# A state-space convolution followed by a gated MLP: the K matmul's moving operand laid out anew, the parameter loads split by chunk, and the order of work before the loop changed

## The chip, the cores and the metric

One core of one Trainium2 chip. The time is device microseconds of one execution, and lower is better. The kernel before takes 380.85 us (median of 16 executions, 379.3 to 383.0). TensorE (PE in the profile) does the matmuls, VectorE is DVE, ScalarE is ACT, GpSimd is POOL.

## The reference

```python
def _A_ref(u, A_re, A_im, B_re, B_im, C_re, C_im, log_dt, Dskip):   # u: 1 x 2048 x 640, parameters 640 x 192
    dt = jnp.exp(log_dt)[:, None]
    logdA = dt * (A_re + 1j * A_im)
    dB = dt * (B_re + 1j * B_im)
    l = jnp.arange(L)
    P = jnp.exp(logdA[:, :, None] * l[None, None, :])
    K = jnp.einsum("dn,dnl,dn->dl", Cc, P, dB).real
    ...                                     # y = causal convolution of u with K along L, by FFT
    return y + u * Dskip

h = x + _A_ref(_layernorm(x), ...)                                   # x is A_u
h2 = h + (silu(_layernorm(h) @ w1) * (_layernorm(h) @ w3)) @ w2      # 640 -> 1536 -> 640
```

All inputs and the output are bf16.

## The kernel before

The work falls into three parts. First, for three chunks of channels (256, 256 and 128 of the 640), the kernel K is built: with a tap number l = 16 j + i, `at` holds w z^j and `bt` holds exp(alpha i), and `k_mm` multiplies them so that the sum over n is the matmul's contraction. `k_evac` (ACT) takes the product from PSUM, and `k_dft` transforms it to frequencies. Secondly, the first tiles of the layer norm and of the transform of u are made. Thirdly, a loop over eight tiles does the inverse transform, the second layer norm and the MLP.

I call what belongs to the K matmuls of chunk 0, 1 and 2 stage 0, 1 and 2. ACT and DVE build the operands of one stage while PE multiplies those of the stage before. `w_mul` makes w, and `w_lanes` (ACT, after transposes on PE) copies it to where `at` needs it. `a_chain` (DVE) builds `at` in five steps, which I call a-steps. `b_first` and `b_rest` (ACT) and `b_mul` (DVE) build `bt`. `kf_evac` takes the frequencies from PSUM, product(c) multiplies those of tile c with those of K, and `h_add` adds a tile's result to the residual.

The matmul and its eviction:

```python
def k_mm(h, at, bt, kc, b):
    ...                                                   # x = cw // 8, 48 for a chunk of 256
        la = mkap(at[p0:p0 + pn], part * JJ * cw + col, [[astr, pn], [x, P]])
        rb = mkap(bt[p0:p0 + pn], part * II * CWM + col, [[bstr, pn], [x, 2], [CWM, II], [2 * x, 4]])
        T.matmul(pk[:, half, gi * P:(gi + 1) * P], lhsT=la, rhs=rb, ...)
    ...                                                   # 32 matmuls make one block

def k_evac(h, pk, kc, b):
    for c2 in range(2):
        src = pk[:].rearrange("p h (g c x) -> p h g c x", g=4, c=2)[:, :, :, c2, :]
        ...
        S.mul(out=dst, in_=src, mul=mask[:, c2:c2 + 1])
```

`la` is the stationary operand and `rb` the moving one. The innermost step of `rb` is 2x = 96 elements.

The order of the program (in the traces each engine's instructions stand in this order: DVE in the kernel before has alpha(0) at 10.04 us, w_mul(0) at 11.53, alpha(1) at 18.51):

```python
alpha(0)                            # DVE: alp = dt * (A_re, A_im), in lanes, from PSUM
c_scale(0); c_scale(1); c_scale(2)  # ACT: csd = dt * C
ze0 = z_exp(0)
w_mul(0, V); w_mul(2, G)            # w = (dt C) B: chunk 0 on DVE, chunk 2 on GpSimd
zs0 = z_sin(0); w_lanes(0)
alpha(1); alpha(2); tables()
b_first(0, bt0, "sin")              # ACT
z_mul(0, zs0, ze0)                  # DVE from here
...                                 # two a-steps, w_mul(1), third a-step, b_mul(0)
for b in range(nb[0]):              # stage 0: four blocks
    pk = k_mm(0, at0, bt0, kc, b)
    if b < len(IGS):
        stg.append(b_rest(1, bt1, "sin", IGS[b]))    # ACT: operands of stage 1
    k_evac(0, pk, kc, b)
...                                 # a_chain(1) on DVE
pb = k_dft(0, kc)
kf_evac(0, pb, "SSSS")
...
zs2 = z_sin(2); b_first(2, bt2, "sin")               # ACT: operands of stage 2
stg = [b_rest(2, bt2, "exp", ig) for ig in IGS]
...
warm(30, at1[:, 0:512])             # 30 dummy matmuls
for b in range(nb[1]):              # stage 1: four blocks
    pk = k_mm(1, at1, bt1, kc, b)
    k_evac(1, pk, kc, b)
pb = k_dft(1, kc)
...                                 # stage 2, layer norm of tiles 0 and 1, k_dft(2)
run(product(0))
...                                 # first inverse tiles, h_add and norm, twice
run(product(1))
for c in range(2, NPRE + 1):
    lst[c] = ln1_stats(c, G)
    if c < NPRE:
        ulns[c] = ln1_apply(c, lst[c]); skip(c, ulns[c])
        for f in range(NFT): fwd_evac(c, f, fwd_mm(ulns[c], f))
for c in range(NC):                 # the loop
    ...
```

## Time and profile before

| | before |
|---|---|
| median, us | 380.85 (16 executions) |
| profiled execution, us | 380.38 (span of the trace 378.4) |
| mean granted TensorE clock | 0.864 |
| PE / DVE / ACT / POOL busy, us | 308.6 / 267.1 / 155.1 / 36.8 |

The shares are averages over stages with different limits, so the reading goes by stretches. Here is the busy time by stretch for stage 0, the stretch before the loop, and the loop. The columns are the stretch in us, its length, then the busy time and the number of instructions of PE, of PE's weight loads, of DVE, ACT and POOL, then the granted clock, the DMA share and GB/s.

```profile
54.82:77.70 22.88, 22.88 (x128) 13.55 (x129) 22.67 (x35) 19.32 (x40) 0.00 (x0) 0.50 0.00 1
147.50:179.50 32.00, 10.77 (x63) 6.26 (x60) 27.10 (x79) 6.47 (x11) 1.56 (x8) 0.69 0.20 62
179.50:378.00 198.50, 188.33 (x1607) 154.40 (x1604) 139.42 (x309) 51.91 (x84) 27.98 (x96) 1.00 0.04 14
```

In stage 0 PE is full, but DVE (22.67 of 22.88) and ACT (19.32) nearly are as well: if PE gets faster there, the others take over soon. In the second stretch only DVE is nearly full. The third is PE's.

### The profile page before, as it was taken

The numbers are of one execution on the slowest core, as the hardware profiler recorded it, in microseconds if no ns is written. First come the engines' busy times: TensorE is split into PE (matmuls) and PEld (weight loads), VectorE is DVE, ScalarE is ACT, GpSimd is POOL, SyncE is SP. The second block draws the span as 40 slices with busy tenths as digits, with TensorE's granted clock in tenths as the row PEclk, the third lists the DMA queues.
The fourth block names the chain that finished last, engine by engine and source line by source line (L and its number), as shares of the span: only waits on it lengthen the run. The fifth ranks groups of instructions, "written<-read, shape, count | busy, mean of one in ns | idle before, by whom it ended". The sixth has DMA issues, their size and how long they took to land.

```text
span 378.4 us, 7036 instructions
## 1 busy us (share of the span) xinstructions
PE 308.6 (82%) x2907; PEld 227.6 (60%) x2907; DVE 267.1 (71%) x584; ACT 155.1 (41%) x317; POOL 36.8 (10%) x124
## 2 busy tenths in 40 slices
PE   1424929989998898204989989989899899998996
PEld 0212315574656656102877878868778778787884
DVE  3589999986994003897687888888879586783222
ACT  2999999818931134102351240421503402213030
POOL 1400000000000000001140230220321101001000
PEclk9999965556855559955999999999999999999999
DMA  8846000000004702400000001000000010000100
GB/s 185 283 126 126 2 0 0 2 2 3 0 3 131 289 0 75 138 0 0 3 1 36 2 0 36 0 9 30 1 19 17 2 36 0 20 17 2 36 0 35
DMA packets 12009, 15.74 MB, mean 42 GB/s; under 512 B 4426, under 2 KB 10570, under 8 KB 11850
## 3 DMA queue, kind: packets, MB, share of 16 engines
q1 hardware_dynamic: 10000, 14.57, 12.4%
q10 hardware_dynamic: 1978, 0.74, 0.8%
q8 instruction: 22, 0.36, 0.4%
q14 instruction: 9, 0.07, 0.1%
HBM read 12.42 MB, written 2.88 MB: 40 GB/s over the span
## 4 chain that ended last, share of the span: by engine, by line
PE 71%; DVE 20%; ACT 3%; DMA 3%; issue 1%; POOL 0%; ACTq 0%; DVEq 0%
PE ps L566 25%; PE ps L296 15%; PE ps L579 14%; PE ps L325 5%; PE ps L531 4%; PE ps L402 3%; DMA par_bi<-in_A_B_im_dram 3%; DVE st L374 3%; PE ps L343 2%; DVE at L279 2%; DVE at L274 2%; DVE tt L276 2%; ACT sg L571 1%; ACT kc L314 1%; DVE xl L545 1%
## 5 line engine op out<-in xcount | busy, mean ns | idle before, releaser
L571 ACT ACTIVATE sg<-ps 128x512 bf16<-128x512 f32 x48 | 28.7, 597 | 131.9 <-PE ps L566 131.9
L296 PE MATMUL ps<-bt,at 128*128 128x128 bf16 (+1 forms) x320 | 57.3, 406 | 7.7 <-DVE bt L260 7.7
L566 PE MATMUL ps<-xt,w1sb 128*128 128x256 bf16 x480 | 60.5, 273 | 0.0
L566 PE MATMUL ps<-xt,w3sb 128*128 128x256 bf16 x480 | 60.2, 273 | 0.0
L572 DVE TENSOR_TENSOR hm<-sg,ps 128x512 bf16<-128x512 bf16 x48 | 32.9, 685 | 36.1 <-ACT sg L571 35.7
L579 PE MATMUL ps<-w2sb,hm 128*128 128x320 bf16 x384 | 53.5, 299 | 0.0
L296 PEld LDWEIGHTS <-at 128*128 128x128 bf16 (+1 forms) x320 | 34.0, 148 | 30.5 <-DVE bt L260 8.2
L566 PEld LDWEIGHTS <-w1sb 128*128 128x128 bf16 x480 | 46.9, 98 | 7.3
L566 PEld LDWEIGHTS <-w3sb 128*128 128x128 bf16 x480 | 47.0, 98 | 5.4
L579 PEld LDWEIGHTS <-hm 128*128 128x128 bf16 x384 | 37.6, 98 | 14.2
L402 PE MATMUL ps<-uln,ft 128*128 128x320 bf16 x128 | 23.5, 332 | 12.4 <-DVE uln L387 11.3
L365 POOL TENSOR_TENSOR ta<-rs 128x2 f32<-128x2 f32 x26 | 7.4, 285 | 228.7 <-DVE rs L363 227.7
L374 DVE BATCH_NORM_STATS2 st<-xs 128x6 f32<-128x320 bf16 x64 | 27.9, 477 | 0.5
L409 ACT CAST vt<-ps 128x640 bf16<-128x640 f32 x32 | 20.9, 694 | 14.9 <-PE ps L402 14.9
L402 PEld LDWEIGHTS <-ft 128*128 128x128 bf16 x128 | 13.4, 107 | 19.8 <-DVE uln L387 11.6
L586 DVE TENSOR_TENSOR ot<-ps,xs 128x640 bf16<-128x640 f32 x16 | 13.2, 824 | 15.7 <-PE ps L579 15.7
L314 ACT ACTIVATE kc<-ps,mask 128x512 bf16<-128x512 f32 x20 | 12.6, 682 | 23.5 <-PE ps L296 23.4
L325 PE MATMUL ps<-kc,wt 32*128 32x64 bf16 (+1 forms) x768 | 18.6, 264 | 4.2 <-ACT kc L314 2.7
L343 PE MATMUL ps<-at,ident 128*128 128x512 bf16 x70 | 19.3, 446 | 2.5 <-DVE at L279 2.5
L338 DVE CAST kf<-ps 128x128 bf16<-128x128 f32 x2 | 0.5, 286 | 29.2 <-ACT kf L336 29.2
L325 PEld LDWEIGHTS <-wt 32*128 32x128 bf16 x768 | 17.8, 115 | 5.4 <-issue 5.4
L231 ACT ACTIVATE bt<-alp 128x384 bf16<-128x384 f32 (+1 forms) x45 | 20.8, 461 | 0.0
(104 smaller groups left out, 398.5 us busy)
## 6 DMA issues: line engine op xcount, KB each, us to landing
xs<-in_A_u_dram SPq DMA_DIRECT2D x4, 640.0 KB, 9.8
out_dram<-ot SPq DMA_DIRECT2D x16, 160.0 KB, 1.8
wt<-ftd SPq DMA_DIRECT2D x4, 512.0 KB, 6.7
w1sb<-in_B_w_dram SPq DMA_DIRECT2D x1, 1920.0 KB, 8.7
w3sb<-in_B_w_dram SPq DMA_DIRECT2D x1, 1920.0 KB, 13.1
w2sb<-in_B_w_dram SPq DMA_DIRECT2D x1, 1920.0 KB, 9.6
ftd<-ft SPq DMA_DIRECT2D x1, 256.0 KB, 2.6
par_ar<-in_A_A_re_dram SPq DMA_DIRECT2D x1, 240.0 KB, 5.7
```

Source lines behind the costliest of these rows:

```text
L231: S.activation(out=dst, in_=alp[h][:, 1, :], func=ACT.Sin, scale=-float(i))
L296: T.matmul(pk[:, half, gi * P:(gi + 1) * P], lhsT=la, rhs=rb, start=first, stop=last, tile_position=((p0, 0) if n1 else None), skip_group_ ...
L314: S.mul(out=dst, in_=src, mul=mask[:, c2:c2 + 1])
L325: T.matmul(pb[blk][:, f * 2 * cg:(f + 1) * 2 * cg], lhsT=wt[32 * blk:32 * blk + 32, i, f * P:(f + 1) * P], rhs=rb, start=(i == 0 and f == ...
L343: T.matmul(pw[:, 0, :], lhsT=ident[:], rhs=rhs, start=True, stop=True)
L374: V.bn_stats(out=st[:, q, :], in_=src[:, q * (D // 2):(q + 1) * (D // 2)])
L402: T.matmul(pv[:, q, 0:D // 2], lhsT=ft[:, k, f * P:(f + 1) * P], rhs=uln[:, k, q * (D // 2):(q + 1) * (D // 2)], start=(k == 0), stop=(k = ...
L409: S.copy(out=vts[c][:, f // 2, f % 2, :].rearrange("p (q d) -> p q d", q=2), in_=pv[:, :, 0:D // 2])
L566: T.matmul(pg[:, b, u * TB:(u + 1) * TB], lhsT=w[:, kt, fb * P:(fb + 1) * P], rhs=xts[c][:, kt, :], start=(kt == 0), stop=(kt == DT - 1))
L571: S.activation(out=sg[:], in_=pg[:, 0, :], func=ACT.Silu)
L572: V.tensor_tensor(out=hms[c][:, 2 * fp:2 * fp + 2, :], in0=sg[:].rearrange("p (u t) -> p u t", u=2), in1=pg[:, 1, :].rearrange("p (u t) -> ...
L579: T.matmul(po[:, q, 0:D // 2], lhsT=hms[c][:, fb, k * P:(k + 1) * P], rhs=w2sb[:, fb, q * (D // 2):(q + 1) * (D // 2)], start=(fb == 0), s ...
```

## The change

The intent has four parts. (1) The channels of a group are laid side by side in `bt`, so that the K matmul's moving operand reads eight neighbours at a time. This needs `alp` in a second order (a second pass of `alpha` for chunks 0 and 1) and makes `k_evac` read every second f32. (2) The loads are split by chunk, chunk 0 first, and c_scale(0) goes from ACT to GpSimd, so that the work starts earlier; on DVE, alpha(1) and alpha(2) move behind the first two a-steps, and the third a-step moves ahead of w_mul(1). (3) The 30 dummy matmuls go, the 40 ahead of stage 0 become 24 that stand earlier in the program but run later, since they read the last a-step and a part of `bt` that is multiplied late, and ACT builds stage 2's operands ahead of `kf_evac(0)`. (4) The statistics of tiles 2 and 3 move ahead of product(0), and the transform of tile 2 goes between the two `h_add`s.

The diff, cut to its core:

```diff
-    for nm, src, q in (("ar", A_A_re, nc.sync), ("cr", A_C_re, nc.scalar), ...):
-        q.dma_start(out=t[:], in_=src.rearrange("(s p) n -> p s n", p=P))
+    for h, cd in enumerate(CHUNKS):
+        nc.scalar.dma_start(out=ldcol[:, s0:s0 + ns], in_=A_log_dt[...].rearrange("(p s) -> p s", s=ns))
+    load(nc.sync, "ar", 0)
+    load(nc.sync, "ai", 0)
+    load(nc.scalar, "cr", 0)
+    load(nc.scalar, "ci", 0)
+    load(nc.sync, "br", 0)
+    load(nc.sync, "bi", 0)
+    for h in (1, 2):
+        for nm in ("ar", "ai", "cr", "ci", "br", "bi"):
+            load(nc.sync, nm, h)
...
-                S.mul(out=csd[:, part, s, :], in_=par[nm][:, s, :], mul=dtcf[:, s:s + 1])
+                if h == 0:
+                    G.tensor_scalar(out=csd[:, part, s, :], in0=par[nm][:, s, :], scalar1=dtcf[:, s:s + 1], ...)
+                else:
+                    S.mul(out=csd[:, part, s, :], in_=par[nm][:, s, :], mul=dtcf[:, s:s + 1])
...
-            rb = mkap(bt[p0:p0 + pn], part * II * CWM + col, [[bstr, pn], [x, 2], [CWM, II], [2 * x, 4]])
+            rb = mkap(bt[p0:p0 + pn], part * II * CWM + 8 * col, [[bstr, pn], [CWM, II], [1, 8]])
...
-            src = pk[:].rearrange("p h (g c x) -> p h g c x", g=4, c=2)[:, :, :, c2, :]
+            src = pk[:].rearrange("p h (g x c) -> p h g x c", g=4, c=2)[:, :, :, :, c2]
...
-    alpha(0)
+    alpha(0, "(m g)")
     c_scale(0)
+    ze0 = z_exp(0)
+    w_mul(0, V)
+    alpha(0, "(g m)")
+    zs0 = z_sin(0)
+    w_lanes(0)
     c_scale(1)
     c_scale(2)
...
-    alpha(1)
-    alpha(2)
...
     at0 = run(a0, 2)
+    alpha(1, "(m g)")
+    alpha(2, "(g m)")
+    run(a0, 1)
     inverse_table()
     w_mul(1, V)
+    alpha(1, "(g m)")
...
+    warm(14, last_a(0, at0))
+    warm(10, bt0[:, 0, IGS[1][-1], 0:CWM])
...
-    warm(40, at0[:, 0:512])
...
+    zs2 = z_sin(2)
+    bt2 = b_tile(2)
+    b_first(2, bt2, "sin")
     pb = k_dft(0, kc)
     kf_evac(0, pb, "SSSS")
...
-    zs2 = z_sin(2)
-    bt2 = b_tile(2)
-    b_first(2, bt2, "sin")
...
-    warm(30, at1[:, 0:512])
...
     pb = k_dft(2, kc)
+    skip(0, ulns[0])
+    ulns[1] = ln1_apply(1, lst[1])
+    lst[2] = ln1_stats(2, G)
+    skip(1, ulns[1])
+    lst[3] = ln1_stats(3, G)
...
         tr_evac(0, k, tp)
+        if k == 0:
+            ulns[2] = ln1_apply(2, lst[2])
+            for f in range(NFT):
+                fwd_evac(2, f, fwd_mm(ulns[2], f))
     run(product(1))
-    for c in range(2, NPRE + 1):
...
+    skip(2, ulns[2])
```

## The prediction

> **What bounds the kernel now.** I read the page's slices first (is one engine always the bound?), then the chain that ended last in order of time, then the timeline and the busy time by stretch where the chain changes engine.
>
> ```profile
> PE   1424929989998898204989989989899899998996
> DVE  3589999986994003897687888888879586783222
> ACT  2999999818931134102351240421503402213030
> PEclk9999965556855559955999999999999999999999
> ```
>
> One digit is 9.46 us. After slice 19 (180 us) PE is full at full clock: 199 us of matmuls that the diff leaves alone. Before it there are four stages with different bounds: ACT and DVE both full (slices 1 to 5), PE at half clock (6 to 15), then DVE with PE empty (16 to 18). The chain, cut to its large pieces:
>
> ```profile
> 2.33 9.85 DMA par_bi<-in_A_B_im_dram
> ...
> 22.02 1.50 DVE zs L212 x3
> ...
> 54.82 22.94 PE ps L296 x125
> 77.78 1.28 ACT kc L314 x2
> 79.10 7.24 PE ps L325 x256
> 86.34 8.96 PE ps L343 x30
> 95.31 22.75 PE ps L296 x121
> ...
> 128.33 11.40 PE ps L296 x63
> ...
> 148.27 0.82 DVE z L516
> ...
> 175.07 4.45 PE ps L402 x16
> ```
>
> So the end is set in turn by the parameter load; DVE without a gap from 22.02 to 54.8; the K matmuls (L296), 57.1 us in three stages; 8.96 us of dummy matmuls (L343) that delay stage 1 although its inputs were ready at about 84.2; and a DVE stretch from 148.3 to 179.5. Why is L296 slow?
>
> ```profile
> 54.82 3.37 PEld L296 LDWEIGHTS <-at 128*128 128x128 bf16 x16 [8.16 <-DVE bt L260]
> 58.58 1.55 PEld L296 LDWEIGHTS <-at 64*128 64x128 bf16 x16 [0.40 <-issue]
> 60.53 3.36 PEld L296 LDWEIGHTS <-at 128*128 128x128 bf16 x16 [0.41 <-issue]
> ...
> 20.95 1.03 PE L126 MATMUL ps<-ident,ft 128*128 128x128 bf16 x8
> ```
>
> Sixteen full matmuls take 58.58-54.82 = 3.76 us, 235 ns each; the sixteen 64-row ones, two side by side, 1.95 us, 244 ns a pair. Eight 128-column transposes of contiguous data take (1.03-0.31)/7 = 103 ns each. L296's moving operand (bt) steps 96 elements between inner columns. That it is the read and not the clock:
>
> ```profile
> 95.30:97.00 1.70, 1.70 (x10) 1.09 (x8) 1.70 (x5) 1.70 (x7) 0.00 (x0) 1.00 0.00 0
> 103.00:105.00 2.00, 2.00 (x12) 1.15 (x12) 2.00 (x4) 1.71 (x5) 0.00 (x0) 0.50 0.00 0
> ```
>
> The first columns are PE busy time and count, the third from the end the clock. Stage 1 starts at clock 1.00 and falls to 0.50, yet takes 22.75 us against 22.94 for stage 0, all at 0.50.
>
> [...] The new moving operand reads 8 consecutive bf16[...]. [...] the change makes k_evac read every second f32, and no row of this trace has such a read. [...] The trace shows 1.00 and 0.50 only; stage 0 stayed at 0.50. [...]
>
> **The change, part by part.**
>
> *Loads and start.* Chunk 0's six arrays (98 KB each) go first and the transpose for dt is gone. Now par_ar lands at 6.9, par_ai at 8.9, and alpha(0) starts at 10.04. New: ldb is still needed (landed 5.04 us), three small exps of about 0.4 us, dtcol, dtcf: alpha(0) at about 6.5 to 8.0. ze0 (1.33) to 9.35, table load (1.28) to 10.6, zs0 (2.77) to 13.4; before, zs0 ended at 18.26. Beside this four GpSimd scales (estimate 0.6 us each) end at about 9, w_mul(0) (about 3.1) at 12.2, the second alpha(0) (1.45) at 13.7. So z_mul(0) starts at about 13.7 instead of 22.02.
>
> *DVE to the first K matmul.* From the timeline: z_mul 1.50, two a-steps 5.03, alpha(1) and alpha(2) 2.37, third a-step 5.34, gt 0.69, w_mul(1) 3.06, alpha(1) again 1.45, two a-steps 10.67, b_mul 6.47: 36.6 us, against 32.8 before. k_mm(0) starts at 13.7+36.6 = 50.3 (was 54.82), gain 4.5. The doubled alphas give back 3.8 of 8.3.
>
> *ACT becomes the bound.* After w_mul(1) (31.7) and its transposes (1.0), w_lanes(1) starts at 32.7 (was 34.63). To the end of ze2 the old timeline has 20.74 us: 53.5. Table load 1.28, then three groups of five sin/cos pairs (5 x 0.92 = 4.6) with a k_evac (1.27) after each and one more: 18.9. End 73.7 (was 79.06). PE's four blocks, at 16 x 107 + 8 pairs x 110 = 2.6 us instead of 5.72, fit in between: the first two wait for nothing, the others for an eviction. So of stage 0's 12.5 us of saved matmul only about 1 reaches the path: ACT would end there anyway.
>
> *Stage 1.* The 8.96 us of L343 go. k_dft(0) 7.3 to 81.0; DVE: z_mul(1) 1.5, a_chain(1) 21.1, b_mul(1) 7.1 from 50.3 gives 80.0. Two blocks run, then their evictions wait for ACT: zs2 2, b_first(2) 9.1, kf_evac 1.2, table 1.28, b_rest(2) 3.92 after 73.7 gives 91.2. Evictions at 92.5 and 93.7, blocks three and four to 97.7, last eviction 99.0 (was 119.4): gain 20.4.
>
> *Stage 2.* k_dft(1) 7.3 plus most of the 1.4 us issue gap that it had beside the weight loads: 107.3 (was 128.3). k_mm(2) 2 x 2.6 instead of 11.4: 112.5. The first fwd_mm 4.1, k_dft(2) 3.8, kf_evac 0.8: product(0) at about 121.3 (was 148.27), gain 27.0. DVE has its layer norm statistics done by then: b_mul(2) ends about 96, and four statistics, two applies and two skips are about 16 us.
>
> *The DVE stretch.* Statistics of tiles 2 and 3 have moved before it; apply(2) and fwd_mm(2) now come between the two h_adds. Counted from product(0): h_add and norm 0 end at 10.3 (as before), apply(2) 11.1, h_add and norm 1 15.6, product(1) (6.7) 22.3. The first inverse matmul of the loop needs product(1): 22.3, against 181.94-148.27 = 33.7 before. gu(0,0) fits before it, from about 17. Gain 11.4. After that every hm is ready before its buffer is wanted, so PE runs as before.
>
> Sum: 27.0+11.4 = 38.4. I take 2 off for a cold first gu (20 matmuls at 213 instead of 109 ns, partly in a wait) and for slower strided reads or writes. 381-36.4 = 344.6; I say 344.5.
>
> **Rivals.** (a) The stationary operand, still strided, takes over. For: its LDWEIGHTS last 148 ns against 98 for contiguous ones at full clock. Against: they overlap the matmuls. If each pitch is 148, a block takes 3.5 us, but only four blocks or so are on the path: +4, 348. If the pitch stays at 235, stage 0 still ends near 74.5, stages 1 and 2 lose 12.5: 357. (b) The strided PSUM read makes ACT's 20 evictions 1.5 times as long; some 14 lie on the path where ACT is the bound: +4 to +5, 349. (c) The clock: packed matmuls and the re-placed warm-ups bring k_dft(1) to 60 ns per four instead of 110: -3.5, 341; or PE idles more while it waits for ACT, and the loop starts cold: +3. (d) The start is no earlier (more DMA issues, slow GpSimd scales): up to +4, since DVE's and then ACT's sequence shifts with it.
>
> **Range and chances.** Even with (a) at its worst the result is some 6% faster, since the dummies' 9 us and the reordering's 11.4 don't depend on it. (a), (b) and (d) lengthen, (c) goes both ways: 335 to 357. Faster 0.96, same 0.03, slower 0.01.
>
> **What would show it.** Right: L296 pitch near 107 ns in a block; alpha(0) near 6.5 us, z_mul(0) near 14; L314 following L228 without gaps in stage 0 and waits of PE for ACT there; no L343 between k_dft(0) and k_mm(1); product(0) near 121; about 23 us from it to the first loop L531. Wrong: L296 staying over 200 ns; L314 near 1 us; k_mm(0) starting after 53; or the loop's 199 us growing because DVE falls behind.

The 107 and 213 ns in it, for 128 and 256 columns at the slow clock, follow from the kernel before as an estimate: its dummy matmuls of 512 columns start 427 ns apart at clock 0.50 (86.7 to 90.9 us), and a quarter and a half of that are 107 and 213. The kernel after shows both at 0.50: 107 in stage 0, where pairs of 64-row matmuls start mostly 104 to 105 apart, and 213 in the loop's first group. For GpSimd's scales (estimate 0.6 us) the kernel before has only GpSimd's two-input f32 products of 192 elements, 0.55 to 0.86 us.

## The result, and the profile after

The kernel after takes 348.03 us (median of 11 executions, 347.55 to 350.41). The ratio to the kernel before is 0.9148, with a 95% interval of 0.9127 to 0.9170. Ratios here are the mean time of one kernel's fast runs over that of the other's fast runs of the same rounds, so they are not quite the ratio of the medians that I quote.

The profiled execution was the slowest of the 11 (350.41 us, span 348.5). I come back to that, because a second profile of the same kernel (a_again below, span 346.0) shows where it lost its 2.5 us.

The page of the kernel after, the slices of PE and of its clock (one digit is 8.7 us):

```profile
PE 264.8 (76%) x2860; PEld 212.2 (61%) x2860; DVE 271.6 (78%) x582; ACT 155.5 (45%) x315; POOL 43.1 (12%) x136
...
PE   2510346339468885779999998998998998998995
...
PEclk9999999555665678889999999999999999999999
```

PE is busy 43.8 us less than before, DVE 4.5 us more, and POOL 6.3 us more. PE reaches its full stretch at slice 18, which is 157 us instead of 180. In slices 7 and 8 (61 to 78 us) PE now has 3s and in slice 10 (87 to 96 us) a 4, where it had 8s and 9s: faster matmuls were in part exchanged for waiting.

The timeline of PE after, K matmuls (now L331) and transforms (now L360). The columns are start, time, engine and line, and in brackets the idle time just before with what ended it:

```profile
55.65 3.74 PE L331 MATMUL ps<-bt,at 128*128 128x128 bf16 x64 [0.35 <-DVE bt L295]
66.05 2.88 PE L331 MATMUL ps<-bt,at 128*128 128x128 bf16 x32 [6.65 <-ACT kc L349]
...
78.70 7.24 PE L360 MATMUL ps<-kc,wt 32*128 32x64 bf16 x256 [4.03 <-ACT kc L349]
85.87 4.84 PE L331 MATMUL ps<-bt,at 128*128 128x128 bf16 x64
98.30 5.28 PE L331 MATMUL ps<-bt,at 128*128 128x128 bf16 x64 [7.59 <-ACT kc L349]
104.94 7.24 PE L360 MATMUL ps<-kc,wt 32*128 32x64 bf16 x256 [1.35 <-ACT kc L349]
113.81 5.76 PE L331 MATMUL ps<-bt,at 128*128 128x128 bf16 x64 [1.63 <-DVE uln L427]
```

Two blocks (x64) take 3.74 us instead of some 11.4. At half clock, one block (x32) takes 2.88 us. But PE now waits for ACT's evictions: 6.65 us ahead of the third block of stage 0, 7.59 us ahead of the third block of stage 1. Stage 0's transform starts at 78.70 us, where it started at 79.10 before: of the saved matmul time and of the earlier start, only 0.4 us has arrived there. Stage 1's transform starts at 104.94 (119.40 before).

The last step goes from product(0) on DVE to the loop's first inverse matmul, which waits for product(1). The first two lines are the kernel before, the others the kernel after (L577 is its inverse matmul; one matmul of that group had run at 147.84):

```profile
148.27 0.82 DVE L516 TENSOR_TENSOR z<-vt,kf 128x1280 bf16<-128x1280 bf16 x1
181.78 1.25 PE L531 MATMUL ps<-xf,gt 128*128 128x320 bf16 x8
...
128.71 0.82 DVE L562 TENSOR_TENSOR z<-vt,kf 128x1280 bf16<-128x1280 bf16 x1
150.23 1.86 PE L577 MATMUL ps<-xf,gt 128*128 128x320 bf16 x7 [2.10 <-DVE xf L569]
```

That is 21.5 us, where the kernel before took from 148.27 to 181.78, 33.5 us.

The start did not go as intended. The first line is ACT; the others are DVE up to the first a-step:

```profile
5.00 1.28 ACT L150 ACT_TABLE_LOAD   x1 [5.00 <-DMA ldcol<-in_A_log_dt_dram]
7.43 1.44 DVE L189 TENSOR_TENSOR alz<-ps,dtl 128x512 f32<-128x512 bf16 x3
9.92 0.77 DVE L208 TENSOR_TENSOR w<-csd,par_br 128x384 f32<-128x384 f32 x1 [1.05 <-POOL csd L198]
13.37 2.18 DVE L189 TENSOR_TENSOR alp<-ps,dtl 128x512 f32<-128x512 bf16 x3
15.58 1.49 DVE L247 TENSOR_TENSOR zs<-zs,ze 128x768 bf16<-128x768 bf16 x3
17.66 0.72 DVE L311 TENSOR_TENSOR tt<-at,zs 128x384 bf16<-128x384 bf16 x1
```

z_mul(0) (L247) starts at 15.58 us instead of 22.02, 6.4 us earlier. Yet the first K matmul starts at 55.65, 0.8 us later than before. Two things show in the lines: the second alpha pass takes 2.18 us although the same work in the first order takes 1.44, and an a-step's product takes 0.72 us. Before, the same product took half of that:

```profile
24.10 0.35 DVE L276 TENSOR_TENSOR tt<-at,zs 128x384 bf16<-128x384 bf16 x1
```

The end of stage 0 hangs on another line, ACT's w_lanes(1), from which ACT then works without a gap up to the first eviction. First the kernel before, then the kernel after with its first eviction:

```profile
34.63 2.04 ACT L188 COPY wl<-ps 128x512 bf16<-128x512 bf16 x6
...
37.32 2.05 ACT L215 COPY wl<-ps 128x512 bf16<-128x512 bf16 x6 [4.44 <-PE ps L165]
64.73 1.27 ACT L349 ACTIVATE kc<-ps,mask 128x512 bf16<-128x512 f32 x2
```

It comes 2.7 us later than before, and ACT is idle for 4.44 us ahead of it: it waits for the transposes of w_mul(1)'s result, and DVE begins w_mul(1) at 33.08 us instead of 29.20, since the third a-step now stands ahead of it and alpha(1) and alpha(2) no longer fall into DVE's idle time.

Milestones of one profiled execution each, in us (the K matmul's start in stage 0, the start of the transforms of stages 0 and 1, product(0), and the loop's second inverse tile; from there to the end all of them take 193.3 to 193.5 us). Four of the experiments below are set beside them:

| kernel | first K matmul | k_dft(0) | k_dft(1) | product(0) | second inverse tile |
|---|---|---|---|---|---|
| before | 54.82 | 79.10 | 119.40 | 148.27 | 185.05 |
| b_packed | 54.76 | 75.20 | 107.02 | 129.70 | 167.01 |
| a_strided | 55.48 | 79.73 | 112.25 | 142.95 | 167.56 |
| a_oldloop | 55.54 | 78.58 | 105.20 | 128.27 | 164.25 |
| after | 55.65 | 78.70 | 104.94 | 128.71 | 155.04 |
| a_best1 | 53.06 | 76.20 | 97.45 | 120.87 | 145.50 |

### The profile page after: what moved, and what is told of

The parts are those of the page before. It is cut to its first block, busy times and chain, and to the rows that moved or that the text cites. A ratio compares the mean times of both kernels' runs of the same rounds, so it can differ in the third digit from the quotient of the medians.

```text
span 348.5 us, 6968 instructions
## 1 busy us (share of the span) xinstructions
PE 264.8 (76%) x2860; PEld 212.2 (61%) x2860; DVE 271.6 (78%) x582; ACT 155.5 (45%) x315; POOL 43.1 (12%) x136
## 3 DMA queue, kind: packets, MB, share of 16 engines
HBM read 12.42 MB, written 2.88 MB: 44 GB/s over the span
## 4 chain that ended last, share of the span: by engine, by line
PE 53%; DVE 32%; ACT 6%; DMA 5%; issue 2%; POOL 1%; SPq 0%; DVEq 0%
PE ps L612 27%; PE ps L625 15%; PE ps L577 5%; DVE at L314 4%; DVE at L309 4%; DVE tt L311 4%; DVE st L414 3%; DMA wt<-ftd 2%; DVE bt L295 2%; DVE bt L294 2%; PE ps L442 2%; PE ps L331 2%; ACT sg L617 1%; PE ps L360 1%; DVE xl L591 1%
## 5 line engine op out<-in xcount | busy, mean ns | idle before, releaser
L612 PE MATMUL ps<-xt,w1sb 128*128 128x256 bf16 x480 | 61.2, 275 | 0.8 <-ACT xt L601 0.8
L331 PE MATMUL ps<-bt,at 128*128 128x128 bf16 (+1 forms) x320 | 25.4, 283 | 19.1 <-ACT kc L349 17.1
L331 PEld LDWEIGHTS <-at 128*128 128x128 bf16 (+1 forms) x320 | 22.9, 159 | 21.8 <-issue 20.4
L405 POOL TENSOR_TENSOR ta<-rs 128x2 f32<-128x2 f32 x28 | 9.4, 337 | 197.6 <-DVE rs L403 196.5
L632 DVE TENSOR_TENSOR ot<-ps,xs 128x640 bf16<-128x640 f32 x16 | 13.2, 825 | 15.7 <-PE ps L625 15.7
L360 PE MATMUL ps<-kc,wt 32*128 32x64 bf16 (+1 forms) x768 | 18.5, 264 | 6.3 <-ACT kc L349 5.4
L360 PEld LDWEIGHTS <-wt 32*128 32x128 bf16 x768 | 17.8, 115 | 7.0 <-issue 6.9
L309 DVE TENSOR_TENSOR at<-at,zs 128x1536 bf16<-128x1536 bf16 (+3 forms) x30 | 20.3, 677 | 0.1
L311 DVE TENSOR_TENSOR tt<-at,zs 128x1536 bf16<-128x1536 bf16 (+3 forms) x30 | 20.3, 677 | 0.0
L577 PE MATMUL ps<-xf,gt 128*128 128x320 bf16 x112 | 18.4, 308 | 2.1 <-DVE xf L569 2.1
L314 DVE TENSOR_TENSOR at<-at,tt 128x1536 bf16<-128x1536 bf16 (+3 forms) x30 | 19.0, 674 | 0.5
```

The source lines that it names most:

```text
L309: V.tensor_tensor(out=av[:, part, :, o0:o0 + w, :], in0=src, in1=z4[:, 0].broadcast_to([P, 4, w, cw // 4]), op=ALU.mult)
L311: V.tensor_tensor(out=tv[:, part], in0=src, in1=z4[:, 1].broadcast_to([P, 4, w, cw // 4]), op=ALU.mult)
L314: V.tensor_tensor(out=dst, in0=dst, in1=tv[:, 1 - part], op=(ALU.add if part else ALU.subtract))
L360: T.matmul(pb[blk][:, f * 2 * cg:(f + 1) * 2 * cg], lhsT=wt[32 * blk:32 * blk + 32, i, f * P:(f + 1) * P], rhs=rb, start=(i == 0 and f == ...
L577: T.matmul(py[:, q, 0:D // 2], lhsT=gt[:, f, k * P:(k + 1) * P], rhs=xx[c][:, f // 2, f % 2, q * (D // 2):(q + 1) * (D // 2)], start=(f == ...
L612: T.matmul(pg[:, b, u * TB:(u + 1) * TB], lhsT=w[:, kt, fb * P:(fb + 1) * P], rhs=xts[c][:, kt, :], start=(kt == 0), stop=(kt == DT - 1))
```

## The experiments

Twelve kernels ran, in four calls; the kernels of one call ran on one chip and shared seven runs of the kernel before. Each has four executions of its own. The names that begin with b are the kernel before with one edit, those with a the kernel after with one edit, except a_again (no edit) and a_best1 (three).

### b_packed: the packed read alone

```diff
-            rb = mkap(bt[p0:p0 + pn], part * II * CWM + col, [[bstr, pn], [x, 2], [CWM, II], [2 * x, 4]])
+            rb = mkap(bt[p0:p0 + pn], part * II * CWM + 8 * col, [[bstr, pn], [CWM, II], [1, 8]])
-            src = pk[:].rearrange("p h (g c x) -> p h g c x", g=4, c=2)[:, :, :, c2, :]
+            src = pk[:].rearrange("p h (g x c) -> p h g x c", g=4, c=2)[:, :, :, :, c2]
```

It is wrong, since `bt` isn't laid out for it. The comparison doesn't notice a K in the wrong order, and can't vouch for K in the kernel after either (a far too large constant, in a_nopool below, it did notice). The same instructions run in the same order as with a right K.

> The kernel before with only the moving read of the K matmuls made contiguous (8 neighbouring elements per step, and the eviction reading every second element as in the changed kernel). Wrong result on purpose: the coefficients behind are in the old order. Theory: the pitch of a full K matmul falls from 235 to about 107 ns, but the time follows ACT's order. From the trace of before: ACT is ready for stage 0 at 56.7 us and needs 18.9 us, so stage 0 ends near 75.6 instead of 79.1; stage 1's evictions wait for ACT's work on chunk 2 and end near 108 instead of 119.4; stage 2 saves about 6. About 363.5 us, 17 less than before. Rival: the saved matmul time (57 to 26 us) counts in full: 350 us.

Measured: 363.04 us, ratio 0.9542 (0.9508 to 0.9575): 17.4 us faster than the 380.4 of the kernel before. PE's timeline of b_packed:

```profile
62.55 2.58 PE L296 MATMUL ps<-bt,at 128*128 128x128 bf16 x32 [2.31 <-ACT kc L314]
```

A block takes 2.58 us instead of 5.72, and PE waits for ACT's evictions already in stage 0, with every other part of the change absent. The table shows where the gain is: 3.9 us to k_dft(0), 12.4 to k_dft(1), 18.6 to product(0). So 18.6 of the 19.6 us that the kernel after has gained at product(0) come with the read alone.

### a_strided: all but the packed read

The reverse of the first pair of lines of that diff, in the kernel after; wrong in the same way.

> The changed kernel with only the old strided moving read of the K matmuls put back. Wrong result on purpose. Theory: pitch 235 ns; stage 0 ends about 1 us later (ACT hides the rest), stage 1 6.5 later, stage 2 5.6 later: about 348 + 13 = 361 us. Rival: the pitch counts in full, 57 minus 26 = 31 us more: 379 us. Second rival: the stationary operand's stride is what costs, then nothing changes: 348 us.

Measured: 363.53 us, ratio 0.9547 (0.9508 to 0.9587), 15.5 us slower than the kernel after. The eviction still reads every second f32 and the stationary operand is as in the kernel after, so the moving read alone makes this:

```profile
55.48 22.89 PE L331 MATMUL ps<-bt,at 128*128 128x128 bf16 x128 [0.35 <-DVE bt L295]
```

Stage 0 is again 22.89 us long. Its transform starts only 1.0 us later than in the kernel after (79.73 against 78.70): there the matmuls were hidden behind ACT, as predicted. The other 13.2 us at product(0) come in stages 1 (6.3) and 2 (6.9).

### b_nodummy: the 30 dummy matmuls taken out of the kernel before

```diff
-    warm(30, at1[:, 0:512])
```

> The kernel before without its second group of 30 dummy matmuls, which lay on the chain that ended last with 8.96 us. Result right. Theory: two blocks of stage 1 start 9 us earlier, but their evictions stand behind ACT's work on chunk 2 in ACT's order (until 103.5 us), so stage 1 ends 2 to 3 us earlier only: about 378 us. Rival: the chain's 9 us come off: 372 us.

Measured: 380.04 us, ratio 0.9983 (0.9953 to 1.0014): no difference shown. The prediction had counted these 9 us as a gain that would stay even if the stationary operand took over as the bound. PE's timeline of b_nodummy:

```profile
86.32 11.49 PE L296 MATMUL ps<-bt,at 128*128 128x128 bf16 x64
104.81 11.47 PE L296 MATMUL ps<-bt,at 128*128 128x128 bf16 x64 [7.00 <-ACT kc L314]
```

The first two blocks start 8.8 us earlier (95.14 before), and then PE waits 7.00 us for an eviction. ACT's order has 15 exponentials of stage 2 ahead of the first eviction of stage 1. In the kernel before ACT does them until 103.5 and evicts then:

```profile
99.64 3.92 ACT L225 ACTIVATE stg<-alp 128x192 bf16<-128x192 f32 x15
103.46 1.25 ACT L314 ACTIVATE kc<-ps,mask 128x512 bf16<-128x512 f32 x2
```

So the dummies stood in a place where PE would have waited anyway. Of the 1.8 us that were left at k_dft(1) (117.64 against 119.40), nothing is seen at product(0) (148.42 against 148.27).

### a_oldloop: the old order before the loop

```diff
-    lst[2] = ln1_stats(2, G)
     skip(1, ulns[1])
-    lst[3] = ln1_stats(3, G)
...
-        if k == 0:
-            ulns[2] = ln1_apply(2, lst[2])
-            for f in range(NFT):
-                fwd_evac(2, f, fwd_mm(ulns[2], f))
     run(product(1))
+    lst[2] = ln1_stats(2, G)
+    ulns[2] = ln1_apply(2, lst[2])
     skip(2, ulns[2])
+    for f in range(NFT):
+        fwd_evac(2, f, fwd_mm(ulns[2], f))
+    lst[3] = ln1_stats(3, G)
```

> The changed kernel with the old order before the main loop: statistics, apply and forward matmuls of tile 2 and statistics of tile 3 again after the second product. Result right. Theory: about 10.4 us more (33.7 from the first product to the loop's first inverse matmul instead of 21.5, less nothing else), 358.5 us. Rival: the DVE work moved ahead only moved the wait, 0 to 4 us more: 348 to 352.

Measured: 359.74 us, ratio 0.9449 (0.9422 to 0.9475): 11.7 us slower than the kernel after, where the prediction had 11.4 for this part. From product(0) to the first inverse matmul of the loop it takes 32.7 us:

```profile
128.27 0.82 DVE L560 TENSOR_TENSOR z<-vt,kf 128x1280 bf16<-128x1280 bf16 x1
160.98 1.25 PE L575 MATMUL ps<-xf,gt 128*128 128x320 bf16 x8
```

Together the runs make a chain in which each link adds one part of the change, or a group of parts: 380.4 (before), 363.04 with the packed read (17.4), 359.74 with all but the loop's order (3.3 more), 348.03 with that order too (11.7 more). The 3.3 us hold the new start, the second alpha passes, the dummies, ACT's new order, and the layer norm's new order ahead of k_dft(2). The table shows that they are a loss and a larger gain: at k_dft(0) a_oldloop is 3.4 us behind b_packed (78.58 against 75.20), so the new start costs time there, and from k_dft(0) to k_dft(1) it needs 26.6 us instead of 31.8. Which part of the change makes that gain was not tested one by one.

### a_evac: the evictions of stage 1 ahead of stage 2's operands on ACT

```diff
-    b_first(2, bt2, "sin")
+    b_first(2, bt2, "sin", 1, 10)
...
-    stg = [b_rest(2, bt2, "exp", ig) for ig in IGS]
...                                   # b_mul(2) goes behind the loop below
     for b in range(nb[1]):
         pk = k_mm(1, at1, bt1, kc, b)
         k_evac(1, pk, kc, b)
+        if b < 2:
+            b_first(2, bt2, "sin", 10 + 3 * b, 13 + 3 * b)
+        elif b == 2:
+            stg.append(b_rest(2, bt2, "exp", IGS[0]))
+        else:
+            stg += [b_rest(2, bt2, "exp", ig) for ig in IGS[1:]]
```

> The changed kernel with another order on ACT only: stage 1's evictions are put between ACT's sin and exp work for chunk 2 instead of behind all of it. Result right. Theory: in the changed kernel PE stands idle for 7.6 us in stage 1 (90.7 to 98.3) because the eviction of its first block comes after ACT's work on chunk 2, which ends at 97.0. With the eviction in turn, PE's four blocks run through from 85.9 to about 95.7 and stage 1 ends near 97 instead of 104.9: 6 to 8 us less, about 341 us. Rival: chunk 2's B table then comes late and stage 2 waits for it: 346 to 348.

Measured: 343.59 us, ratio 0.9009 (0.8985 to 0.9034): 4.4 us faster than the kernel after. This is the test that ACT's order, and not PE, sets stage 1. PE's timeline of a_evac:

```profile
85.72 7.06 PE L331 MATMUL ps<-bt,at 128*128 128x128 bf16 x96
93.02 1.85 PE L331 MATMUL ps<-bt,at 128*128 128x128 bf16 x32 [0.23 <-ACT kc L349]
99.79 7.24 PE L360 MATMUL ps<-kc,wt 32*128 32x64 bf16 x256 [4.92 <-ACT kc L349]
```

The four blocks now run nearly without a wait, and stage 1's transform starts at 99.79 instead of 104.94. The gain is less than expected since I had put a table load and five exponentials ahead of the last eviction: it could start at 94.9 and started at 98.50, and PE waits 4.92 us for it.

### a_nopool: GpSimd's w_mul(2) taken out

```diff
-    w_mul(2, G)
+    G.memset(wdn[:, :, DT - 1:DT, :], 0.01)
```

Wrong on purpose (relative error 66), to take GpSimd's work away from beside DVE's first a-steps.

> The changed kernel without GpSimd's w_mul for chunk 2 (its result is a constant instead; wrong on purpose). In the changed kernel DVE's first chain steps took about twice their time (0.70 instead of 0.35 us) from 17.7 to 20.8 us, just while GpSimd did these multiplications. Theory: they contend; without them the steps take 0.35 us again, the first K matmul starts 2.2 us earlier (53.4 instead of 55.65), and the time falls by about 2 us: 346. Rival: the slow steps come from something else (ACT reading at the same time, or the tables' transfer), then nothing changes.

Measured: 346.81 us, ratio 0.9098 (0.9071 to 0.9125), whose interval ends just below that of the kernel after (0.9127) and overlaps that of a_again. The trace decides. DVE's timeline of a_nopool, the same step as the 0.72 us above, and PE's first K matmul:

```profile
17.54 0.35 DVE L312 TENSOR_TENSOR tt<-at,zs 128x384 bf16<-128x384 bf16 x1
...
53.45 3.75 PE L332 MATMUL ps<-bt,at 128*128 128x128 bf16 x64 [0.35 <-DVE bt L296]
```

The step is back at 0.35 us, as expected, and the first K matmul starts 2.2 us earlier, at 53.45 (0.1 of it was there at z_mul(0) already); 1.2 us of it are left at the end. So DVE's slower steps beside `w_mul(2)` are a cost of the new order. Before, `w_mul(2)` ran from 13.6 us on beside the end of DVE's w_mul(0), two of whose steps took 0.90 and 0.79 us instead of 0.55, and then beside DVE's idle time; now it runs beside the a-chain, which is on the path. This part of the early start's loss is shown; what in w_mul(2) slows DVE was not tested apart.

### a_cact: c_scale(0) back on ACT

```diff
-                if h == 0:
-                    G.tensor_scalar(out=csd[:, part, s, :], in0=par[nm][:, s, :], scalar1=dtcf[:, s:s + 1], ...)
-                else:
-                    S.mul(out=csd[:, part, s, :], in_=par[nm][:, s, :], mul=dtcf[:, s:s + 1])
+                S.mul(out=csd[:, part, s, :], in_=par[nm][:, s, :], mul=dtcf[:, s:s + 1])
```

> The changed kernel with chunk 0's C scaling back on ACT instead of GpSimd. Result right. The four GpSimd scales took 0.77 us each (7.62 to 10.63) and w_mul(0) waited for them; ACT was idle from 7.3 to 8.9. Theory: ACT does them in 1.5 us in that gap, w_mul(0) starts about 1 us earlier, and so does the first K matmul: about 347 us. Rival: ze0 on ACT is pushed back by as much, or DMA landing is the limit: no change.

Measured: 347.00 us, ratio 0.9109 (0.9081 to 0.9136). The time alone doesn't separate it from the kernel after. In the trace w_mul(0) starts at 8.82 us instead of 9.92, the first K matmul at 54.28 instead of 55.65, and k_dft(0) at 77.30 instead of 78.70. GpSimd's four scales took 0.77 us each (I had predicted 0.6), and they were on the path.

### a_alphawr: the second alpha pass writes in order

```diff
+            dt1 = dv[r, :, :, gs].broadcast_to([r.stop - r.start, 2, 8, n])
+            if order == "(g m)":
+                dst, src, dt1 = (v.rearrange("p a m g -> p a g m") for v in (dst, src, dt1))
-            V.tensor_tensor(out=dst, in0=src, in1=dv[r, :, :, gs].broadcast_to([r.stop - r.start, 2, 8, n]), op=ALU.mult)
+            V.tensor_tensor(out=dst, in0=src, in1=dt1, op=ALU.mult)
```

> The changed kernel with the second alpha multiplication walking its operands in the order of its output, so that DVE writes next to next and reads PSUM with a stride instead. Result right. In the changed kernel these groups took 2.16 to 2.18 us against 1.45 for the same elements in the old order. Theory: the strided f32 write is what costs, so they take 1.45 again, 0.7 us less before z_mul(0) and 1.1 later: about 346.5 us. Rival: a strided PSUM read costs as much: no change, 348.

Measured: 349.54 us, ratio 0.9161 (0.9136 to 0.9186), no gain. My theory was that the strided write makes the pass long. It fails: with the write in order and both reads strided instead, the pass takes 2.09 us where it had 2.18, and the pass in the first order 1.44. One side has to be strided in this pass, and either costs some 0.7 us here.

### a_again: the kernel after once more, as a control

> The changed kernel once more, unchanged, as a control beside the next two and for a second trace (the first trace is of an execution of 350.4 us, 2.4 above the median). Expected 348 us; the trace should have the same order of stages, with a difference of about 2 us somewhere in the clock's phases or the issue gaps.

Measured: 347.98 us, ratio 0.9125 (0.9091 to 0.9159), the profiled execution 347.84. Up to product(0) it is 0.75 us ahead of the kernel after's profile (127.96 against 128.71). The rest of the 2.5 us comes at the start of the loop, where the inverse matmul is back to its usual length:

```profile
149.22 1.32 PE L577 MATMUL ps<-xf,gt 128*128 128x320 bf16 x8
```

Between 150 and 155 us the granted clock was 1.00 here and 0.66 in the kernel after's profile, in which the gate and up group behind that inverse matmul took 3.1 us instead of 2.2 (here the slow one was the group ahead of it, with 3.9 us). It is one kernel, so this is a difference between executions, and no property of the change.

### a_ldcol: the small log-dt loads behind chunk 0's loads

```diff
-    for h, cd in enumerate(CHUNKS):
-        nc.scalar.dma_start(out=ldcol[:, s0:s0 + ns], in_=A_log_dt[...].rearrange("(p s) -> p s", s=ns))
     load(nc.sync, "ar", 0)
...
     load(nc.sync, "bi", 0)
+    for h, cd in enumerate(CHUNKS):
+        nc.sync.dma_start(out=ldcol[:, s0:s0 + ns], in_=A_log_dt[...].rearrange("(p s) -> p s", s=ns))
```

> The changed kernel with the three small loads of log dt (128 rows of 2 or 4 bytes each) moved from the head of ACT's queue to SP's queue, behind chunk 0's six loads. Result right. In the changed kernel both queues stop issuing between 2.5 and 4.5 us, par_bi and par_ci go out only then, and ACT's first table load starts at 5.00, waiting for the small loads. Theory: the small loads with their many rows hold the queues; moved, ACT's table load starts near 2.5, alpha(0) near 6 instead of 7.43. GpSimd's scales still need log dt, so the first K matmul gains 0.5 us or so: 347.5 us. Rival: the queues stop for another reason (the broadcast load of log dt), then alpha(0) stays near 7.4.

Measured: 349.96 us, ratio 0.9162 (0.9117 to 0.9207), 2.0 us slower than a_again (the fastest of the one and the slowest of the other meet, 348.52 and 348.54; in the traces it is 1.0 us behind at k_dft(0)). The table load did move, from 5.00 us to 1.66. (The three small loads take SP's queue 2.56 us to issue, from 3.06 us on, where each of its four loads of chunk 0 takes 0.42 to 0.43.) But alpha(0) starts later, at 8.29 instead of 7.43:

```profile
8.21 0.17 DVE L154 CAST dtcf<-dtcol 128x5 f32<-128x5 bf16 x1 [4.02 <-ACT dtcol L152]
8.29 1.45 DVE L189 TENSOR_TENSOR alz<-ps,dtl 128x512 f32<-128x512 bf16 x3
```

I had overlooked that this small cast stands ahead of alpha(0) in DVE's order, and that it needs exactly the load that I had put last.

### a_nowarm: the 24 dummy matmuls ahead of stage 0 taken out

```diff
-    warm(14, last_a(0, at0))
-    warm(10, bt0[:, 0, IGS[1][-1], 0:CWM])
```

> The changed kernel without its two groups of dummy matmuls (14 and 10) before stage 0. Result right. Theory: they bring the clock to 1.00 for the first two blocks (1.87 instead of about 2.5 us each), but ACT takes the first block only at 64.7 us, five us after both are done: no change, 348 us. Rival: the stage needs the warm clock, 1 to 3 us more.

Measured: 350.41 us, ratio 0.9186 (0.9152 to 0.9221), 2.4 us slower than a_again; the four executions of each don't overlap. The first two blocks of stage 0 take 4.99 us instead of 3.74, and k_dft(0) starts at the same time all the same (78.48 against 78.56), since ACT sets it. The loss is seen later, at k_dft(1) (105.00 against 104.27) and at product(0) (129.93 against 127.96). In stage 2 PE has one idle time more whose end the profile gives to no other engine:

```profile
117.28 3.32 PE L331 MATMUL ps<-bt,at 64*128 64x128 bf16 x39 [0.59 <-issue]
```

Idle times of this kind, of up to 1.7 us, stand in nearly every trace of this case, inside or just ahead of stage 2. In the kernel before one is at 125.41 to 126.84, and in the kernel after one is at 112.18 to 113.81 (there the profile names DVE's uln, which the K matmul doesn't read). In the four traces where I looked (before, after, a_evac, a_nowarm) a packet of the instruction queue, 16 KB, starts 0.7 to 1.9 us before each; but in the kernel after the packets at 86.11 and 115.26 us have no such idle time behind them. So packet and idle time are no more than a coincidence in time here; what makes these gaps is not shown, and no run tests it. Why the dummies are worth 2.4 us stays open.

### a_best1: a version from what the experiments showed

It joins the diffs of a_evac and a_cact, and holds GpSimd's w_mul(2) back until DVE's first two a-steps are done, by a copy of one element that DVE writes then:

```diff
-    w_mul(2, G)
...
     alpha(1, "(m g)")
+    hold = early.tile([P, 1], F32, name="hold")
+    G.tensor_copy(out=hold[:], in_=alz[1][:, 0, 0:1])
+    w_mul(2, G)
     alpha(2, "(g m)")
```

> The changed kernel with what the runs found: stage 1's evictions in turn on ACT (alone 343.6 us), chunk 0's C scaling back on ACT (alone 347.0), and GpSimd's w_mul for chunk 2 held back until DVE multiplies from PSUM (a one-element copy makes it wait). Result right. Theory: the gains add, since the first shortens stage 1 and the others start DVE's chain 1 to 2 us earlier: 4.4 + 1 + 0.5 to 1.2 off 348, about 342 us. Rival: stage 1 is then bound by PE's k_dft(0) or by DVE's B table, and the earlier start is lost there: 343.5 us.

Measured: 341.05 us, ratio 0.8945 (0.8901 to 0.8988), correct. It is 7.0 us faster than the kernel after and 40 us faster than the kernel before. PE's timeline of a_best1:

```profile
53.06 3.77 PE L328 MATMUL ps<-bt,at 128*128 128x128 bf16 x64 [0.19 <-DVE bt L292]
...
83.37 9.38 PE L328 MATMUL ps<-bt,at 128*128 128x128 bf16 x128
97.45 7.24 PE L357 MATMUL ps<-kc,wt 32*128 32x64 bf16 x256 [4.70 <-ACT kc L346]
```

The first K matmul is 2.6 us earlier than in the kernel after, and stage 1's four blocks run through in one piece. The 4.70 us wait for the last eviction is still there: a next version would put that eviction ahead of the table load (not run).

## Why the prediction was right or wrong, point by point

The predicted 344.5 us missed the median by 3.5 us, 1%, and the range held it. The steps are less good than the sum.

**The packed read: right.** At half clock the full matmuls of stage 0's last blocks start 107 ns apart, exactly as predicted; at full clock they start 64 to 70 ns apart, but for the first of a run. The 235 of the prediction is a mean over sixteen that includes the turn to the next group; from one start to the next it was mostly 225 to 233 before. One comparison of the prediction proves less than it says: it sets the eight transposes (103 ns) beside matmuls at the slow clock, but the trace of the kernel before has no record of the clock ahead of 39.9 us, and the views print 1.00 there. That 107 ns go with the half clock is shown by the kernel after (66.00 to 74.70 us, clock 0.50). Rival (a), the strided stationary operand as the new bound, is false: its loads last 159 ns on average, and yet a pair of load and matmul passes every 64 ns. Rival (b), the slow strided read of PSUM, is false as well: a pair of evictions takes 1.27 us before and after. Of rival (c), the transform at 60 ns per four did not come: in k_dft(1) of the kernel after the fours start 110 ns apart at clock 1.00 (105.0 to 106.0 us) and at 0.50 alike.

**ACT becomes the bound in stage 0: right.** From w_lanes(1) (37.32 us) to the last eviction (78.64) ACT needs 41.3 us, and the prediction had 41.0. That is why the 13 us of matmul time saved in stage 0 come to 1.0 at its end (a_strided).

**The earlier start: wrong, and this is the step that failed.** The prediction had alpha(0) at about 6.5 us, z_mul(0) at about 13.7 and the first K matmul at 50.3, a gain of 4.5. The runs show 7.43, 15.58 and 55.65, a loss of 0.8: 5.3 us off. Rival (d) had this with up to 4 us. 1.9 us of it are there at z_mul(0): ACT's table load waits for ldcol until 5.00, GpSimd's scales take 0.77 us instead of 0.6 (a_cact: 1.4 at the first K matmul), and the second alpha(0) takes 2.18 instead of 1.45 us. Then 2.1 us come from DVE's slower steps beside GpSimd's w_mul(2), which weren't in the prediction at all (a_nopool). Another second alpha pass (2.16 instead of 1.45, chunk 1) and alpha(2) (1.24 instead of 0.92) account for 1.0 of the remaining 1.4 us. The delay goes on to the end of stage 0 by way of w_lanes(1), which ACT began at 37.32 us and not at the predicted 32.7: 78.70 where 73.7 was predicted. This step did not merely bring less than predicted, it cost time: with the packed read alone (b_packed) stage 0's transform starts at 75.20, 3.5 us sooner than in the kernel after. Even a_best1, with w_mul(2) held back and without the slow scales, has w_lanes(1) at 34.82 and that transform at 76.20. Putting w_mul(1) ahead of the third a-step again is an obvious next test (not run).

**The dummies: right in what happened, wrong as a reason.** The prediction lists 8.96 us of dummies as delaying stage 1, and says that these 9 us don't depend on rival (a). b_nodummy shows no clear gain from taking them out of the kernel before (0.4 us, within the noise), since the evictions stood behind ACT's 15 exponentials. Stage 1's own sum was right all the same, as it was counted from ACT's end: from k_dft(0) to k_dft(1) 26.2 us against 25.3 predicted (zs2 takes 3.0 us instead of 2: ACT now reads its f32 input with a step of 8, and a cosine of 192 columns takes 0.66 us instead of 0.49; those of b_first(2), which read the same tile in order, take 0.46 to 0.47).

**Stage 2: nearly right.** k_dft(1) to product(0) takes 23.8 us, with 22.3 predicted; the idle time of PE ahead of k_mm(2) stayed whole (1.63 us), and k_mm(2) took 5.76 us instead of 5.2. So product(0) comes at 128.71, 7.4 us later than the 121.3 predicted: 5.0 from stage 0, 0.9 from stage 1, 1.5 here.

**The loop's order: right.** 22.3 us from product(0) to the loop were predicted, 21.5 measured, and a_oldloop puts the part at 11.7 us (11.4 predicted).

**The sum.** Without its allowance of 2 the prediction is 342.6. With product(0) 7.4 later, the loop's start 0.8 sooner after it, and 1.5 for the cold first group, it is 350.7, and the profiled execution took 350.41. The median is 2.4 us below that execution, of which a_again shows the larger part to be the clock at the loop's start, rival (c).

So the gain of 32.8 us has two sources that are shown: the packed read (17.4 when it is added to the kernel before, 15.5 when it is taken from the kernel after) and the loop's order (11.7). The remaining 3.3 to 3.7 us, a loss in stage 0 and a larger gain behind it, were not separated further.

## What to carry to other kernels

Before work is counted as saved, ask what the consumer would be waiting for at that moment: dummy matmuls or slow matmuls that end while another engine still holds the evictions cost next to nothing here (0.4 us in b_nodummy, 1.0 us at the end of stage 0 in a_strided), and the place to gain is that engine's order. An earlier start is worth only what survives the chain up to the engine that bounds the stage, and when an order changes, what DVE does beside GpSimd's work must be checked again (here a product took 0.72 us beside w_mul(2) and 0.35 without it). Ask too which result the bounding engine waits for: the first K matmul was not it, w_lanes(1) was. A step in a matmul's moving operand is worth a look in any tuned kernel (here some 230 ns against 107 at clock 0.50): a few matmuls of the same shape on contiguous data, at the same clock, give the time that it should take.

## What was measured of single instructions

- 128-column matmuls whose moving operand steps 96 elements start some 230 ns apart at clock 1.00 and at 0.50 alike (kernel before, 225 to 234 in stages 1 and 0); with eight neighbours side by side they start 107 ns apart at 0.50 and 64 to 70 ns at 1.00 (kernel after, stage 0, in runs of sixteen but for the first of a run). A stationary operand with a step of 48 elements did not bind, though its loads last 159 ns.
- ACT's eviction of every second f32 takes 1.27 us a pair, the same as the contiguous one of the kernel before.
- On GpSimd a scale of 192 bf16 elements to f32 took 0.77 us, more than the 0.55 us of a two-input f32 product of the same size (0.55 to 0.86 us in the kernel before); ACT did the same scale in 0.44 us.
